# Two tiles at a time to VectorE: handing out the exponentials of an attention kernel in pairs behind group 560

## The chip, the cores and the metric

The kernel runs on one core of one Trainium2 chip. The metric is the device time of one execution in microseconds (us); of several executions the median is given. The core's engines are TensorE (PE in the profile; PEld is its weight load), ScalarE (ACT), VectorE (DVE), GpSimd (POOL) and SyncE (SP, which here issues most DMAs). They run side by side and wait for one another on semaphores only.

## The reference

The input `x` (2048 rows of 512) goes through two branches, and a gate mixes them:

```python
x = A_x
g = _sigmoid((x * gate_w).sum(-1, keepdims=True))
a = _A_ref(x, A_wqkv, A_wo)          # softmax attention, 32 heads of 16
b = _B_ref(x, B_A_re, ..., B_Dskip)  # long convolution with a kernel K(d, l) of 512 x 2048
return g * a + (1 - g) * b
```

The attention is the part that matters here:

```python
scores = jnp.einsum("bhqd,bhkd->bhqk", q, k) * scale
p = _softmax(scores, axis=-1)
o = jnp.einsum("bhqk,bhkd->bhqd", p, v)
```

It has 32 x 2048 x 2048 scores, each of which needs an exponential. The convolution branch builds its kernel K from powers of complex numbers, in 16 blocks of 32 channels, and applies it with matmuls.

## The kernel before, in words

**Tiles, quads, groups.** The scores are cut into 2048 tiles of 128 keys by 512 queries. Four tiles that share the keys and queries and differ in the head make a *quad* (512 quads; 16 quads make a block, 32 blocks). A list `tiles` gives the order in which tiles are worked on, and three consecutive entries are a *group*: 683 groups, the unit of the main loop at the end of `record`. A group's three tiles lie in the three banks of one of two PSUM buffers, `SC0` and `SC1`, which take turns: group g uses `SC[g % 2]`.

**One group's way.** `qk(g)` has TensorE write the three tiles of scores into `SC[g % 2]` (line 701, shown as `SC<-Qm,KT`). `ex(g)` has ScalarE take the exponential of the group, in one ACTIVATE over three tiles (1536 columns) or two (1024), into the ring `ET` or `EX` in SBUF (line 961). `pv(q)` then multiplies a finished quad with the values into the bank `OA`. As there are two buffers, `qk(g + 1)` can start only when group g - 1 has been read out of its buffer, and ScalarE can start group g + 1 only when `qk(g + 1)` is done.

**VectorE's share.** Some groups give their third tile to VectorE. Such a tile is turned into a 16-bit pattern that, read as bfloat16, approximates the exponential (`bits`, line 982, shown as `DZ<-SC`). Three shifted copies of that pattern (`batch`, line 996, shown as `DU<-DZ`, the shifts are in `CUTS`) are summed with it by matmuls (`sums`), which evens the error out. Four tiles of one quad are a *set*: a set covers three quads, of which one (c in the code) goes to VectorE and two (a and b) to ScalarE. Its four VectorE tiles lie in four consecutive groups, one in each, so that ScalarE has four groups of two tiles. The dictionary `vec` holds, for each such group, the number of its set and which of the set's four tiles it has.

**What sets the order.** All of this is planned in Python while the program is built. `Prog` keeps a clock for each engine from a cost given with each instruction; `Sched` holds threads of work (projections, tables of the convolution kernel, its application, outputs) and puts pieces of them between the groups where the clocks leave room. The order on each engine's queue is fixed by this plan. `decide` chooses where a set starts: at a group x, and, behind the last set's start, at a distance of at least 5 groups (the `gap` in `WIN`), or at least 9 (`SL`) where the plan counts as *slow*. It is slow when fewer blocks of the convolution kernel are finished than a line in x asks for:

```python
def win(x):
    slow = done() < KA + (x - KX) / KB
    return next((w for w, (lo, hi, _, gap, *_) in enumerate(WIN) if lo <= x < hi and x >= plan["x"] + (SL if slow else gap)
                 and len(sets) <= (min(x, XR) - RX) / RATE + max(x - XR, 0) / RATE2), None)
```

`done()` is the number of finished blocks (99 once all 16 are finished), `KA` is -2, `KX` is 100 and `KB` is 26. With k blocks finished the plan is slow at groups beyond 100 + (k + 2) x `KB`. A set also starts only in the first 13 quads of a block. `WIN` has two windows: groups 110 to 559 (window 0) and 560 to 677 (window 1); they differ in the number of buffers for VectorE's results.

The finished blocks are seen in the profile by the transposition `Kt<-MB` (line 1402), one for each block. The outputs of rows 0 to 1535 (`MB<-Wo,OnR`, and line 1618) come after the last block has been applied. What follows the last group is a fixed chain: the last quad, normalisation, the last output rows, their DMA.

Of the kernel before, what the change touches and what calls it, by code (L numbers as in the profile page):

```python
# [11 lines left out]
ALU = mybir.AluOpType  # L12
# [37 lines left out]
XS = 128 * DH ** -.5 / math.log(2)  # L50
CUTS = (26, 56, 94)
XB = 128 * (127 - math.log2(5.3794))
# [5 lines left out]
KX = 100  # L58
SL = 9
YQ = 0  # L60
KB = 26
RX = 100
RATE2 = 5.3
XR = 560
# [30 lines left out]
SPILL = 3  # L95
DVCAP = 6
DVK = 14
JS = ((2, 0, 3, 1), (1, 0, 2, 3), (0, 2, 1, 3))
DVL = 14
VW = 136  # L100
VG = 4 * VW + 16
# [2 lines left out]
class Buf:  # L104
# [18 lines left out]
    def int(self, off, dims):  # L123
        return self(off, dims).bitcast(INT32)
# [12 lines left out]
class Prog:  # L137
# [113 lines left out]
    def op(self, eng, fn, R=(), W=(), c=.1, lat=.085, a=0, cfg=None):  # L251
        if self.cap is not None:
            self.cap.append((self.op, (eng, fn, R, W), dict(c=c, lat=lat, a=a, cfg=cfg)))
            return
        if cfg is not None:
            if cfg != self.cfg:
                c += TURN[cfg]
            self.cfg = cfg
        self.act += a
        self.log.append((self.op, self.q, (eng, fn, R, W)))  # L260
        deps = self._deps(eng, R, W)
        i = self.cnt[eng]
        at = self.tm[eng]
        for s, k in deps.items():
            at = max(at, self.fin[(s, k)] + (.03 if s == eng else .05))
        if eng == "PE" and len(self.pt) + 1 >= self.edge():
            at = max(at, self.land())
        self.tm[eng] = at + c
        if eng == "DVE":
            self.busy += c  # L270
        self.fin[(eng, i)] = at + c + lat
        self.cnt[eng] += 1
        w = self._record(eng, fn, deps, eng, i, R, W)
        if eng == "PE":
            b = self.edge()
            self.pt += [at] * (2 + max(w - 1, 0))
            if len(self.pt) > b:
                self.av.append(max(self.pt[b - LEAD] + F1, self.av[-1] + F2))
        return at + c + lat
# [406 lines left out]
def record(nc, p, B, ins):  # L686
# [5 lines left out]
    op, dma = p.op, p.dma  # L692
# [128 lines left out]
    tiles, sets, vec, home, held = [], [], {}, {}, {}  # L821
# [3 lines left out]
    def idle():  # L825
        return max(p.tm["ACT"], p.tm["DVE"]) - p.busy
# [9 lines left out]
    def decide(g):  # L836
        while len(tiles) < min(3 * g + 3, NSL):
            q, x = plan["q"], len(tiles) // 3
            kt = q % 16
            if kt == 0:  # L840
                plan["wait"] = None
            plan["used"] = max(plan["used"], idle() - DVCAP)
            if kt < DVK - 1 and win(x) is not None and idle() - plan["used"] >= WIN[win(x)][4] \
                    and (kt < DVL or not sets or f"dvp{len(sets) - 1}" in sch.flag):
                w = win(x)
                plan["used"] += WIN[w][4]
                plan["x"] = x
                c = q if kt else q + 1
                a, b = [y for y in range(q, q + 3) if y != c]
                own, late = [4 * a + k for k in range(4)] + [4 * b + k for k in range(4)], [4 * c + k for k in JS[len(tiles) % 3]]  # L850
                js = JS[len(tiles) % 3]
                k = 0
                for _ in range(12):
                    if len(tiles) % 3 == 2:
                        vec[len(tiles) // 3] = (len(sets), k)
                        k += 1
                        tiles.append(late.pop(0))
                    else:
                        tiles.append(own.pop(0))
                plan["wait"] = f"dvp{len(sets)}"  # L860
                n = sum(st["w"] == w for st in sets)
                r, ru = f"{w}{n % WIN[w][2]}", f"{w}{n % WIN[w][5]}"
                old = [i for i, st in enumerate(sets) if st["r"] == r]
                olu = [i for i, st in enumerate(sets) if st["ru"] == ru]
                sets.append(dict(js=js, q=c, b=c // 16, w=w, r=r, ru=ru, z=B["DZ" + r], u=[B[f"DU{ru}{k}"] for k in range(len(CUTS))],
                                 old=old[-1] if old else None, olu=olu[-1] if olu else None))
                qs, plan["q"] = [a, b], q + 3
            else:
                tiles.extend(range(4 * q, 4 * q + 4))
                qs, plan["q"] = [q], q + 1  # L870
            for y in qs:
                if y < NQ - 1:
                    todo.append((y, plan["prev"], plan["wait"]))
                plan["prev"] = y
            seat()
            while todo and 4 * todo[0][0] + 3 in home:
                sch.add(pvq(*todo.pop(0)), 0)

    def seat():
        while 3 * len(held) + 3 <= len(tiles) or len(tiles) == NSL and len(held) < NG:  # L880
            g = len(held)
            n = 2 if g in vec else len(slots(g))
            m = NS2 if g >= NSG else NS
            if plan["at"] < NS < plan["at"] + n:
                plan["at"] = NS
            if plan["at"] + n > m:
                plan["at"] = 0
            held[g] = plan["at"]
            for i in range(n):
                home[tiles[3 * g + i]] = held[g] + i  # L890
            plan["at"] = (held[g] + n) % m
# [23 lines left out]
    def at_slot(s):  # L915
        q, j = divmod(tiles[s], 4)
        b, kt = divmod(q, 16)
        return q, j, b, kt, (b % 8) // 2

    def slots(g):  # L920
        return range(3 * g, min(3 * g + 3, NSL))
# [33 lines left out]

    def ex(g):
        sc, e = SC[g % 2], held[g]
        ts = tiles[3 * g:3 * g + (2 if g in vec else 3)]
        n = len(ts)
        E, at = et(e)  # L960
        op("ACT", lambda a: a.activation(E(at, [[1, 512 * n]]), sc(0, [[1, 512 * n]]), AF.Exp, scale=DH ** -0.5),  # L961
           [(sc, i, g) for i in range(n)], [(E, e + i, ts[i]) for i in range(n)] + [(B["tk"], g)], c=.055 + .4267 * n, lat=.105)
        p.tick = max(g - 1, 0)
# [12 lines left out]
            pv_mm(s, *et(home[s]), [(et(home[x])[0], home[x], x) for x in (own if k == 0 else [s])], QUAD if k == 0 else 0)  # L976

    def bits(g):
        i, k = vec[g]
        sc, z = SC[g % 2], sets[i]["z"]  # L980
        yield ("DVE", .6, -1)
        op("DVE", lambda v: v.tensor_scalar(z.u16(512 * k, [[1, 512]]), sc(1024, [[1, 512]]), XS, XB, ALU.mult, ALU.add),  # L982
           [(sc, 2, g)], [(z, k, (i, k))], c=.605)
        sch.mark(f"bits{g}")
        if k == 3:
            sch.add(batch(i), 0)

    def batch(i):
# [705 lines left out]
    for q4 in range(4):  # L1694
        sc = SC[1] if q4 < 3 else MB
# [44 lines left out]
    lack = t0 = bare = 0  # L1740
    for g in range(NG):
        p.q = g
        for i in range(2 if g in vec else len(slots(g))):
            if held[g] + i in ring:
                sch.force(f"pv{ring[held[g] + i] // 4}")
            ring[held[g] + i] = tiles[3 * g + i]
        ex(g)
        sch.mark(f"g{g}")
        sch.mark(f"blk{at_slot(3 * g)[2]}")
        if g + 1 < NG:  # L1750
            decide(g + 1)
            need(g + 1)
            if g - 1 in vec:
                sch.force(f"bits{g - 1}")
            sc = SC[(g + 1) % 2]
            while lack >= 256 and bare:
                n = 512 if lack >= 512 else 256
                for j in range(4):
                    zero((sc, [(sc, 0, ("z", g + 1))]), n, (0, 32 * j), 128, 32, n * ZCOL if j == 0 else 0, n // 4, "C", True)
                lack -= n  # L1760
                bare -= 1
            lack += p.act
            qk(g + 1)
            if g + 1 in vec:
                i = sets[vec[g + 1][0]]["old"]
                if i is not None:
                    sch.force(f"dvp{i}")
                sch.add(bits(g + 1), 0)
        t = p.tm["ACT"]
        want = (FILL if g < REST[3] else FILL2) * (t - t0) / 1.335 + min(max(lack, -256), 768)  # L1770
        t0 = t
        sch.rest = g < REST[3] and g % REST[0] < REST[1]
        if sch.rest:
            want = max(want, REST[2])
        sch.fill(t, t + OVER, want)
        lack = want - p.act
        p.act = bare = 0
        while lack >= 256 and p.tm["PE"] < t + OVER and g < NG - 1:
            z = zbank()
            if z is None:  # L1780
                bare = BARE
                break
            n = 512 if lack >= 512 else 256
            for j in range(4):
                zero(z, n, (0, 32 * j), 128, 32, n * ZCOL if j == 0 else 0, n // 4, "C")
            lack -= n
        p.act = 0
# [27 lines left out]
    for i in range(4):  # L1815
        b, off, sl = banks[i]
# [42 lines left out]
```

## Time and profile before

| | |
|---|---|
| median of 3 runs | 786.94 us (786.87 to 787.43) |
| profiled execution, its own time | 787.2 us |
| its span in the profile | 785.4 us |
| mean granted TensorE clock | 0.997 |
| ScalarE busy | 768.4 us, 98% of the span |
| VectorE busy | 748.7 us, 95% |
| TensorE busy | 689.5 us, 88% |
| VectorE's conversions of score tiles | 372 (93 sets of four) |

The profile is of one execution. A row of the grouped views gives a line, an engine, an operation, what it writes and reads, and the number of instructions, then busy time and the mean duration of one. Where consecutive instructions of ScalarE or VectorE run without a pause, the record of one begins before that of the one before it has ended, so that durations add up to more than the time that passed; the time that one costs is then the distance between two ends.

### The profile page before, as it was taken

The numbers are of one execution on the slowest core, as the hardware profiler recorded it, in microseconds if no ns is written. First come the engines' busy times: TensorE is split into PE (matmuls) and PEld (weight loads), VectorE is DVE, ScalarE is ACT, GpSimd is POOL, SyncE is SP. The second block draws the span as 40 slices with busy tenths as digits, with TensorE's granted clock in tenths as the row PEclk, the third lists the DMA queues.
The fourth block names the chain that finished last, engine by engine and source line by source line (L and its number), as shares of the span: only waits on it lengthen the run. The fifth ranks groups of instructions, "written<-read, shape, count | busy, mean of one in ns | idle before, by whom it ended". The sixth has DMA issues, their size and how long they took to land.

```text
span 785.4 us, 31633 instructions
## 1 busy us (share of the span) xinstructions
PE 689.5 (88%) x14177; PEld 295.3 (38%) x14177; DVE 748.7 (95%) x1307; ACT 768.4 (98%) x694; POOL 11.5 (1%) x21
## 2 busy tenths in 40 slices
PE   7787778788778999989999899989999999889997
PEld 3233332222224544445444455443444444322222
DVE  7999998999999999999999999999999999899996
ACT  7999999999999999999999999999999999999996
POOL 5000000000000000000000000000000000000000
PEclk9999999999999999999999999999999999999999
DMA  9544212302002677674776664775665588721101
GB/s 201 90 108 89 62 40 92 116 31 59 5 8 53 158 178 189 162 205 105 195 177 178 194 158 111 206 193 165 178 143 140 136 194 210 174 48 32 32 15 35
DMA packets 168425, 95.52 MB, mean 122 GB/s; under 512 B 117729, under 2 KB 148834, under 8 KB 167906
## 3 DMA queue, kind: packets, MB, share of 16 engines
q1 hardware_dynamic: 166274, 92.33, 46.1%
q8 instruction: 111, 1.82, 1.0%
q10 hardware_dynamic: 2016, 1.18, 0.7%
q14 instruction: 24, 0.20, 0.1%
HBM read 63.81 MB, written 19.42 MB: 106 GB/s over the span
## 4 chain that ended last, share of the span: by engine, by line
ACT 91%; PE 4%; DVE 3%; DMA 1%; issue 0%; ACTq 0%; DVEq 0%
ACT ET L961 83%; ACT EX L961 8%; PE SC L701 2%; PE OA L701 1%; PE MB L701 1%; DVE DZ L982 1%; DMA Wk<-in_A_wqkv_dram 1%; DVE DU L996 1%; DVE T L1040 0%; DVE Yst L1497 0%; DVE OT L1016 0%; ACTq L705 0%; DVEq L663 0%; DVE KT L798 0%; DVE Kt L1402 0%
## 5 line engine op out<-in xcount | busy, mean ns | idle before, releaser
L961 ACT ACTIVATE ET<-SC 128x1024 bf16<-128x1024 f32 (+1 forms) x614 | 695.7, 1463 | 4.5 <-PE SC L701 3.3
L701 PE MATMUL SC<-Qm,KT 32*128 32x512 bf16 x2048 | 273.4, 385 | 81.2 <-ACT ET L961 70.6
L982 DVE TENSOR_SCALAR DZ<-SC 128x512 uint16<-128x512 f32 x372 | 248.5, 683 | 13.3 <-PE SC L701 11.3
L996 DVE TENSOR_SCALAR DU<-DZ 128x2048 uint16<-128x2048 uint16 x279 | 183.0, 686 | 0.5
L701 PEld LDWEIGHTS SC<-Qm,KT 32*128 32x128 bf16 x2048 | 70.4, 91 | 275.5 <-ACT ET L961 219.0
L701 PE MATMUL OA<-wm 128*32 128x256 bf16 (+3 forms) x862 | 157.3, 340 | 1.2 <-DVE wm L754 1.2
L701 PE MATMUL OA<-ET,VE 128*32 128x512 bf16 x1516 | 158.1, 390 | 0.2
L701 PE MATMUL OA<-DU,VE 128*32 128x512 bf16 x1116 | 105.0, 385 | 0.0
L701 PEld LDWEIGHTS MB<-U,H 128*32 128x32 bf16 x4096 | 83.0, 144 | 22.6 <-issue 11.8
L701 PE MATMUL MB<-U,H 128*32 128x128 bf16 (+7 forms) x4096 | 87.5, 224 | 0.0
L961 ACT ACTIVATE EX<-SC 128x1024 bf16<-128x1024 f32 (+1 forms) x69 | 81.6, 1406 | 0.0
L701 PEld LDWEIGHTS OA<-ET,VE 128*32 128x32 bf16 x1516 | 40.8, 94 | 75.5 <-issue 72.0
L1040 DVE TENSOR_TENSOR T<-B,DT 128x1536 bf16<-128x1536 bf16 x64 | 59.3, 947 | 0.0
L701 PEld LDWEIGHTS MB<-T,Z 128*32 128x32 bf16 x2048 | 46.1, 153 | 12.3 <-issue 7.0
L701 PE MATMUL MB<-T,Z 128*32 128x64 bf16 (+1 forms) x2048 | 48.6, 235 | 0.1
L701 PEld LDWEIGHTS OA<-wm 128*32 128x32 bf16 (+2 forms) x862 | 41.8, 95 | 14.5 <-issue 11.4
L701 PEld LDWEIGHTS OA<-DU,VE 128*32 128x32 bf16 x1116 | 28.8, 96 | 33.9 <-issue 24.2
L701 PE MATMUL OA<-DZ,VE 128*32 128x512 bf16 x372 | 37.2, 384 | 1.0 <-issue 1.0
L1016 DVE STREAM_TRANSPOSE OT<-OA 128x512 f32<-128x512 f32 x32 | 22.7, 709 | 2.8 <-PE OA L701 2.8
L1497 DVE TENSOR_TENSOR Yst<-MB,gt 128x512 bf16<-128x512 f32 x32 | 21.8, 682 | 2.2 <-PE MB L701 1.9
L701 PE MATMUL OA<-EX,VE 128*32 128x512 bf16 x160 | 21.9, 387 | 0.0
L1040 DVE TENSOR_TENSOR ft<-Z,DM 128x1024 bf16<-128x1024 bf16 x32 | 21.3, 676 | 0.0
(145 smaller groups left out, 439.6 us busy)
## 6 DMA issues: line engine op xcount, KB each, us to landing
H<-gm_kd SPq DMA_DIRECT2D x128, 256.0 KB, 3.8
U<-gm_xs SPq DMA_DIRECT2D x128, 134.2 KB, 3.5
T<-B SPq DMA_DIRECT2D x16, 256.0 KB, 3.1
gm_yd<-Yst SPq DMA_DIRECT2D x64, 64.0 KB, 2.9
gm_bd<-B16s SPq DMA_DIRECT2D x3, 1024.0 KB, 4.5
B<-gm_bd SPq DMA_DIRECT2D x12, 256.0 KB, 4.0
gm_kd<-Ks SPq DMA_DIRECT2D x64, 40.0 KB, 3.2
gm_xs<-xP SPq DMA_DIRECT2D x16, 136.0 KB, 3.4
```

Of the source, the lines that this page charges most:

```text
L701: op("PE", lambda t: t.matmul(out(), lhsT(), rhs(), start=start, stop=stop, skip_group_check=True, **kw), R, W, c=c, lat=.15, a=a, cfg=cfg)
L961: op("ACT", lambda a: a.activation(E(at, [[1, 512 * n]]), sc(0, [[1, 512 * n]]), AF.Exp, scale=DH ** -0.5), [(sc, i, g) for i in range(n)] ...
L982: op("DVE", lambda v: v.tensor_scalar(z.u16(512 * k, [[1, 512]]), sc(1024, [[1, 512]]), XS, XB, ALU.mult, ALU.add), [(sc, 2, g)], [(z, k, ...
L996: op("DVE", lambda v, u=u, cut=cut: v.tensor_scalar(u.u16(0, [[1, 2048]]), z.u16(0, [[1, 2048]]), float(cut), None, ALU.add), R, [(u, 0, i ...
L1016: op("DVE", lambda v: v.transpose(OT(512 * w, [[1, 512]]), OA(0, [[1, 512]])), [(OA, 0, b)], [(OT, w, b)], c=.64)
L1040: op(eng, lambda v: v.tensor_tensor(o(), a(), b_(), f), R, W, c=c)
L1497: op("DVE", lambda v, w=w, h=h: v.tensor_tensor(Yst(1024 * w + 4 * h, [[128, R8], [8, 16], [1, 4]]), MB(0, [[1, R8], [R8, 16], [NC, 4]]), ...
```

## The change

Sets in window 1, which starts at group 560, use new patterns of tiles (`PAIRED`). A pattern lists the set's twelve tiles in their order; there are three, for a set that starts at the first, second or third place of a group. In each of them VectorE's four tiles lie in two groups, two in each, in the second and third bank, and one ACTIVATE of one tile (512 columns) is left to ScalarE there. The set's other groups have three tiles for ScalarE. `bits` converts the two tiles in one instruction over 1024 columns, and its planned cost is a formula in the number of tiles (0.604 us for one in place of 0.605). In window 0 the patterns (`SINGLE`) spell out the order that was there before. Apart from that `KB` goes from 26 to 26.6, which moves the line against which the finished blocks are counted, in both windows.

```diff
-KB = 26
+KB = 26.6
...
-JS = ((2, 0, 3, 1), (1, 0, 2, 3), (0, 2, 1, 3))
+SINGLE = ("a0 a1 c2 a2 a3 c0 b0 b1 c3 b2 b3 c1", "a0 c1 a1 a2 c0 a3 b0 c2 b1 b2 c3 b3", "c0 a0 a1 c2 a2 a3 c1 b0 b1 c3 b2 b3")
+PAIRED = ("a0 c1 c2 a1 a2 a3 b1 c0 c3 b0 b2 b3", "c0 c1 a1 a2 a3 a0 c2 c3 b0 b1 b2 b3", "a0 a1 c0 c2 a2 a3 b1 b0 c1 c3 b2 b3")
+RUN = (SINGLE, PAIRED)
...
-                own, late = [4 * a + k for k in range(4)] + [4 * b + k for k in range(4)], [4 * c + k for k in JS[len(tiles) % 3]]
-                js = JS[len(tiles) % 3]
-                k = 0
-                for _ in range(12):
-                    if len(tiles) % 3 == 2:
-                        vec[len(tiles) // 3] = (len(sets), k)
-                        k += 1
-                        tiles.append(late.pop(0))
-                    else:
-                        tiles.append(own.pop(0))
+                js, at = [], {}
+                for t in RUN[w][len(tiles) % 3].split():
+                    if t[0] == "c":
+                        at.setdefault(len(tiles) // 3, []).append(len(js))
+                        js.append(int(t[1]))
+                    tiles.append(4 * dict(a=a, b=b, c=c)[t[0]] + int(t[1]))
+                for y, ks in at.items():
+                    vec[y] = (len(sets), ks[0], len(ks))
...
-            n = 2 if g in vec else len(slots(g))
+            n = act(g)
...
+    def act(g):
+        return 3 - vec[g][2] if g in vec else len(slots(g))
+
...
-        ts = tiles[3 * g:3 * g + (2 if g in vec else 3)]
+        ts = tiles[3 * g:3 * g + act(g)]
...
     def bits(g):
-        i, k = vec[g]
+        i, k, n = vec[g]
         sc, z = SC[g % 2], sets[i]["z"]
-        yield ("DVE", .6, -1)
-        op("DVE", lambda v: v.tensor_scalar(z.u16(512 * k, [[1, 512]]), sc(1024, [[1, 512]]), XS, XB, ALU.mult, ALU.add),
-           [(sc, 2, g)], [(z, k, (i, k))], c=.605)
+        yield ("DVE", .07 + .534 * n, -1)
+        op("DVE", lambda v: v.tensor_scalar(z.u16(512 * k, [[1, 512 * n]]), sc(512 * (3 - n), [[1, 512 * n]]), XS, XB, ALU.mult, ALU.add),
+           [(sc, 3 - n + x, g) for x in range(n)], [(z, k + x, (i, k + x)) for x in range(n)], c=.07 + .534 * n)
         sch.mark(f"bits{g}")
-        if k == 3:
+        if k + n == 4:
             sch.add(batch(i), 0)
```

More of the change, by code (lines that the diff above doesn't have):

```diff
@@ L1742, in record @@
         p.q = g
-        for i in range(2 if g in vec else len(slots(g))):
+        for i in range(act(g)):
             if held[g] + i in ring:
```

## The prediction

> **What bounds the kernel now.** I read the page first: its head, the busy times, the chain that ended last.
>
> ```profile
> span 785.4 us, 31633 instructions
> PE 689.5 (88%) x14177; PEld 295.3 (38%) x14177; DVE 748.7 (95%) x1307; ACT 768.4 (98%) x694; POOL 11.5 (1%) x21
> ACT 91%; PE 4%; DVE 3%; DMA 1%; issue 0%; ACTq 0%; DVEq 0%
> ```
>
> ScalarE is busy 98% and has 91% of the chain; VectorE is close behind at 95%. The chain in order of time (start, length, what) gives the price of one ACTIVATE, as pieces in which ScalarE never waits:
>
> ```profile
> 11.92 1.45 ACT ET L961
> ...
> 13.89 69.84 ACT ET L961 x52
> ...
> 603.15 0.59 DVE DZ L982
> 603.79 0.40 PE SC L701
> 604.21 4.20 ACT ET L961 x4
> ...
> 624.05 1.20 DVE DZ L982 x2
> ...
> 700.37 2.75 ACT EX L961 x3
> ```
>
> The piece of 52 lies before group 110, where all groups have three tiles: 69.84 / 52 = 1.343 us each. The piece at 700.37 is three groups of two tiles: 2.75 / 3 = 0.917. A tile more costs 0.426, so one tile alone should cost 0.917 - 0.426 = 0.491. The first ACTIVATE, with none before it, took 1.45: running on, each saves some 0.10. The grouped rows give the number of each form:
>
> ```profile
> L961 ACT ACTIVATE ET<-SC 128x1536 bf16<-128x1536 f32 x288 | 414.8, 1720 | 2.4 <-PE SC L701 2.2 <-PE OA L701 0.2
> L961 ACT ACTIVATE ET<-SC 128x1024 bf16<-128x1024 f32 x326 | 330.0, 1236 | 2.1 <-PE SC L701 1.1 <-PE OA L701 0.9
> L982 DVE TENSOR_SCALAR DZ<-SC 128x512 uint16<-128x512 f32 x372 | 248.5, 683 | 13.3 <-PE SC L701 11.3
> L961 ACT ACTIVATE EX<-SC 128x1024 bf16<-128x1024 f32 x47 | 51.4, 1270 | 0.0
> L961 ACT ACTIVATE EX<-SC 128x1536 bf16<-128x1536 f32 x22 | 35.1, 1697 | 0.0
> ```
>
> 310 groups of three and 373 of two. The first ends at 11.92 + 1.45 = 13.37; the others cost 309 x 1.343 + 373 x 0.917 = 757.0. Now by stages: from 13.37 to group 110, window 0, window 1, and what follows the last ACTIVATE (us, then busy us of each engine):
>
> ```profile
> 13.37:161.00 147.63, 115.93 (x2286) 43.22 (x2290) 141.68 (x265) 146.87 (x111) 0.32 (x1) 0.99 0.38 90
> 161.00:650.00 489.00, 442.36 (x10001) 207.81 (x9993) 475.87 (x815) 486.14 (x451) 0.00 (x0) 1.00 0.54 141
> 650.00:776.56 126.56, 116.70 (x1772) 38.18 (x1765) 118.87 (x195) 126.56 (x124) 0.00 (x0) 1.00 0.32 79
> 776.56:785.38 8.82, 4.42 (x23) 1.51 (x21) 3.58 (x7) 1.07 (x2) 0.00 (x0) 0.91 0.18 60
> ```
>
> So the span is 13.37 + 757.0 + 8.82 and 6.2 us in which ScalarE starved. The third row matters most: where the new patterns go, ScalarE is busy for all of 126.56 us, and VectorE (the third busy figure, 118.87) has 7.7 us to spare. There time can be won only by giving ScalarE fewer columns, and is lost by any wait of ScalarE.
>
> **The change part by part.** *ScalarE's own work in window 1.* Four of the 372 conversions make a set, 93 sets in all. Of the stretch from 650.00 to 776.56 alone:
>
> ```profile
> L961 ACT ACTIVATE ET<-SC 128x1024 bf16<-128x1024 f32 x63 | 67.4, 1321 | 0.0
> L982 DVE TENSOR_SCALAR DZ<-SC 128x512 uint16<-128x512 f32 x92 | 61.9, 685 | 5.7 <-PE SC L701 4.8
> ```
>
> That is 23 sets (one starts every 5.33 groups in 118, as close as the gap allows, so no further set fits in). A set cost 4 x 0.917 = 3.67 us and will cost 2 x 0.491 + 2 x 1.343 = 3.67: nothing won, nothing lost.
>
> *A wait it adds.* With two buffers, the scores of group g + 1 are written between the end of group g - 1 and the start of g + 1, that is, while ScalarE works on g. From the timeline, at 699 to 701 us:
>
> ```profile
> 699.03 1.34 ACT L961 ACTIVATE ET<-SC 128x1024 bf16<-128x1024 f32 x1
> ...
> 700.42 0.09 PEld L701 LDWEIGHTS SC<-Qm,KT 32*128 32x128 bf16 x1 [0.47 <-ACT ET L961]
> 700.43 0.39 PE L701 MATMUL SC<-Qm,KT 32*128 32x512 bf16 x1
> ```
>
> The ACTIVATE ends at 700.37; the matmuls start 0.06 later and take 0.39; TensorE had stood idle for 0.47, waiting for just this end. In the chain above, matmuls that end at 604.19 release ScalarE at 604.21, 0.02 later (0.04 with the rounding of the rows). So group g + 1 starts 0.47 to 0.49 after the end of g - 1. Over a group of two tiles (0.917) that leaves 0.4 us. Behind the change each group of one tile is followed by one of three (in all three patterns), and one tile lasts 0.491: the next ACTIVATE starts just as that one ends, takes the 1.45 of one that runs alone instead of 1.343, and ScalarE loses (0.47 to 0.49) + 1.45 - 0.491 - 1.343 = 0.09 to 0.11 us. Two such places in each of 23 sets: 46 x 0.10 = 4.6 us, all on the path that ends last. The bounds: nothing, if ScalarE takes a late start without loss; and 0.3 a place (13.8) if TensorE is also busy with one more batch (0.39 long, issued in about 0.2) when the buffer comes free. I take 0.10, as TensorE's idle 0.47 says that it is there in time.
>
> The Trainium skill ("ScalarE: Activation LUTs", section "What ACT_TABLE_LOAD costs") states 186 ns + 0.833 ns per column for an ACTIVATE, and that back-to-back ones overlap by about 93 ns. By that, one tile costs 0.520 in a row instead of my 0.491, the loss is 0.49 + 0.093 - 0.520 = 0.06 a place, an estimate of 2.8 us for the 46. Its two figures fit three tiles alone (1.466 for a measured 1.45) but miss the distance in a row (1.373 for 1.343), so I stay with the rows; the direction is the same.
>
> *VectorE's work.* Two conversions in a row take 1.20 (the row at 624.05). For 1024 columns the nearest rows are float products of 1024 and 512 columns:
>
> ```profile
> L1040 DVE TENSOR_TENSOR ft<-FP,L 128x1024 f32<-128x1024 f32 x8 | 9.6, 1219 | 0.0
> L1040 DVE TENSOR_TENSOR ft<-FP,L 128x512 f32<-128x512 f32 x8 | 5.2, 677 | 0.0
> ```
>
> 512 columns more cost 0.54, so a pair in a row costs 0.60 + 0.54 = 1.14 and saves 0.06, 46 x 0.06 = 2.8 us of VectorE; the bounds are 0 and, were the second half as cheap as the copies over 2048 16-bit columns (0.60), 0.6 a pair. It lies in the stretch where VectorE has 7.7 us to spare and ScalarE none: worth nothing to the time. The other side: a buffer now comes free only when VectorE has read its two tiles. Its instruction can start with the scores, some 0.5 after the end of g - 2, and ends 1.2 later, at 1.7; ScalarE's next need of this buffer (0.49 before the end of g + 1, less the 0.10) is at 1.343 + 0.491 + 1.343 - 0.59 = 2.6. A wait behind one other instruction (0.6 to 0.75) is covered; a wait behind two (1.2) costs some 0.3. I take none.
>
> *KB.* With k blocks of the convolution kernel done, the plan turns slow 0.6 x (k + 2) groups later: 1 to 10 groups. Each set that this brings turns four groups of three into four of two: 4 x 0.426 = 1.70 us less for ScalarE, against 4 x 0.60 conversions and 3 x 0.60 shifted copies, 4.2 us, more for VectorE. That work delays the blocks that the rule counts, and so calls the slow plan back. The last block shows how tight the rule is:
>
> ```profile
> L1402 DVE STREAM_TRANSPOSE Kt<-MB x16: 694/706/718, 248.8 to 628.2; 128x512 f32<-128x512 f32 x16
> ```
>
> Its sixteenth and last record is the last block's. The stretch up to it, for line 961 alone (busy us of ScalarE and the number of its ACTIVATEs):
>
> ```profile
> 0.00:628.20 628.20, 613.88 (x541) 1.00 0.51 129
> ```
>
> So 541 ACTIVATEs have begun by then; the bound for it is 100 + 17 x 26 = 542 and becomes 552.2. The blocks may thus run up to ten groups late. At full density (a set in 5.33 groups, 4 x 0.917 + 1.33 x 1.343 = 5.5 us, 4.2 of them for the set) ten groups leave VectorE 10 x 1.3 / 5.33 = 2.4 us; in a slow stretch (a set in 9, 10.4 us, 6.2 left) 6.9 us. The work put off is 2.4 to 6.9 us, room for 0.6 to 1.6 sets. I take one, 1.7 us; the ends are none and two, and three if VectorE's 13 us of idle time in window 0 can be used. The tables put off by ten groups move their stores, loads and the output matmuls with them; these outputs are through early:
>
> ```profile
> L701 PE MATMUL MB<-Wo,OnR x192: 378/379/391, 697.4 to 763.5; 128*32 128x512 bf16 x192
> ```
>
> 13 us before the last ACTIVATE ends: covered, and beyond that each us late would be a us lost. Nothing else moves: SP, POOL and DMA issues keep their order, and one-tile sets of window 0 keep their instructions.
>
> *The sum.* 787.2 of the profiled execution + 4.6 - 1.7 = 790.1. The median, 786.94, lies 0.26 below that execution: 789.8.
>
> **The rivals.** *The added sets come back to none* (the delayed blocks bring one slow gap more): + 4.6, 791.5. For it: 541 against 542, the rule is a loop. Against it: ten groups of leeway.
>
> *Two sets*, 788.1; *three or more*, 786.4. For it: VectorE's idle 13 us; against it: it is idle in scraps.
>
> *The wait does not form*, the one on the other side: ScalarE takes up group g + 1 while g still runs, and a start 0.1 too late costs nothing, so that the sets alone count: one gives 786.94 - 1.7 = 785.2, faster. It decides where a place costs under (1.70 - 1.57) / 46, practically nothing. For it: ACTIVATEs overlap in the records (the first at 699.03 lasts 1.34 for a cost of 0.917). Against it: the 1.45 of one that starts behind an empty engine.
>
> *VectorE frees the buffer late* in a third of the pairs, 15 x 0.35 = 5 us more: 795. For it: it is busy 94% in window 1. Against it: the 0.9 us of slack, of which one instruction ahead takes 0.75 at most.
>
> The Trainium skill ("VectorE: DVE Perf Modes", section "The TRN2 errata — SBUF-src ops pay a fixed extra latency per instruction") has 120 + columns cycles at 0.96 GHz for a read from PSUM, and advises large tiles, as each pays the fixed part once: 1.19 for a pair instead of 2 x 0.66, an estimate of 5.8 us of VectorE for the 46. It speaks for the change where VectorE sets the end; by the third stage row it does not.
>
> **How the numbers follow.** Chances: the forecast 0.35 (its own range 788.7 to 791); no added set 0.19; two 0.16; three or more 0.07; no wait 0.15; VectorE late 0.08. A change under 0.2% (1.6 us) can hardly be told from none. Faster: 0.15. Within: 0.16 + 0.07 = 0.23. Slower: 0.35 + 0.19 + 0.08 = 0.62. Leaving out the last case and the upper edge of the second, the range is 785.0 to 792.3.
>
> **What would show it.** 46 ACTIVATEs of 128x512, each followed by one of 1536 that lasts about 1.45 where it lasted 1.7, and with its end 1.44 behind the one before; ScalarE's idle or lost time behind group 560 up from under 1 to about 5 us; VectorE's conversions of 1024 columns at 1.2 alone; 376 tiles converted in all (94 sets). It is wrong if those ACTIVATEs end 1.343 apart, if the number of sets differs from 94 by two or more, or if the time before group 560 grows because blocks of the convolution kernel come late.

## The result, and the profile after

The changed kernel takes 796.06 us (794.46 to 800.11, four runs) against 786.9 us: 1.26% slower, ratio 1.0126 with an interval of 1.0103 to 1.0149. A second set of four runs, on another occasion, gave 797.51 us and 1.0144 (1.0128 to 1.0161). The forecast was slower, 789.8 us, with a range up to 792.3; the direction was right, and the step that it forecast is a third of the one that came.

The profiled execution is the slowest of the first four, 800.11 us, with a span of 798.3. Its page, in the lines that answer to those shown of before:

```profile
span 798.3 us, 31726 instructions
PE 695.7 (87%) x14199; PEld 296.4 (37%) x14199; DVE 746.3 (93%) x1261; ACT 774.3 (97%) x694; POOL 11.4 (1%) x21
ACT 77%; PE 10%; DVE 8%; DMA 3%; issue 2%; ACTq 0%; SPq 0%; DVEq 0%
```

ScalarE has as many instructions as before (694), and its share of the chain that ended last falls from 91% to 77%, while TensorE's rises from 4% to 10% and VectorE's from 3% to 8%: ScalarE now waits for others. The grouped rows by form:

```profile
L964 ACT ACTIVATE ET<-SC 128x1536 bf16<-128x1536 f32 x321 | 454.0, 1654 | 7.1 <-PE SC L703 6.1
L964 ACT ACTIVATE ET<-SC 128x1024 bf16<-128x1024 f32 x260 | 257.2, 1182 | 2.0 <-PE SC L703 1.6 <-PE OA L703 0.3
L985 DVE TENSOR_SCALAR DZ<-SC 128x512 uint16<-128x512 f32 x280 | 186.5, 683 | 12.6 <-PE SC L703 10.9
L985 DVE TENSOR_SCALAR DZ<-SC 128x1024 uint16<-128x1024 f32 x46 | 56.5, 1228 | 11.2 <-PE SC L703 10.8
...
L964 ACT ACTIVATE ET<-SC 128x512 bf16<-128x512 f32 x29 | 17.6, 607 | 0.0
L964 ACT ACTIVATE EX<-SC 128x512 bf16<-128x512 f32 x17 | 10.2, 601 | 0.0
```

29 + 17 = 46 ACTIVATEs of one tile, 46 conversions of two. VectorE converted 280 + 2 x 46 = 372 tiles: 93 sets, as before, not 94. So ScalarE's work by the prediction's prices is the same sum in both kernels, 757.0 us, and nearly the whole difference is waiting. To see where, the span is cut at the end of group 559. A row is a stretch of the trace: its start, end and length in us, the busy time of PE, PEld, DVE, ACT and POOL (with the number of instructions), the granted clock, the busy share of the DMA engines and their GB/s. Before:

```profile
13.37:650.33 636.96, 558.62 (x12283) 251.03 (x12283) 617.89 (x1079) 633.34 (x562) 0.32 (x1) 1.00 0.51 130
650.33:776.56 126.23, 116.37 (x1768) 38.18 (x1765) 118.54 (x195) 126.23 (x124) 0.00 (x0) 1.00 0.32 79
```

After:

```profile
13.10:654.19 641.09, 561.31 (x12072) 246.64 (x12072) 616.28 (x1076) 634.32 (x562) 1.22 (x5) 0.99 0.50 124
654.19:790.11 135.92, 120.50 (x2006) 44.08 (x1998) 117.70 (x152) 131.16 (x124) 0.00 (x0) 1.00 0.38 97
790.11:798.31 8.20, 4.20 (x22) 1.50 (x20) 3.58 (x7) 1.07 (x2) 0.00 (x0) 1.00 0.20 65
```

From group 560 on, ScalarE has 30 x 1.343 + 93 x 0.917 = 125.6 us of work before, and 46 x 0.491 + 76 x 1.343 + 0.917 = 125.6 after. It took 126.2 before and 135.9 after: 0.7 us of waits have become 10.3. Ahead of group 560 the work is 757.0 - 125.6, or 631.5 with one decimal more; waits of 5.5 us have become 9.6. The tail (what follows the last ACTIVATE) is 0.6 shorter, the start 0.3. That is 9.7 + 4.1 - 0.9 = 12.9, the distance of the two spans.

A *place* from here on is a group of one tile and the group of three behind it. Two places in a row, from the timeline of the kernel after:

```profile
696.96 2.55 ACT L964 ACTIVATE EX<-SC 128x512 bf16<-128x512 f32 x3
697.12 0.09 PEld L703 LDWEIGHTS SC<-Qm,KT 32*128 32x128 bf16 x1 [0.68 <-ACT ET L964]
...
699.08 0.10 PEld L703 LDWEIGHTS SC<-Qm,KT 32*128 32x128 bf16 x3 [0.20 <-ACT EX L964]
699.08 0.39 PE L703 MATMUL SC<-Qm,KT 32*128 32x512 bf16 x3
699.52 4.13 ACT L964 ACTIVATE ET<-SC 128x1536 bf16<-128x1536 f32 x3
```

The row at 696.96 holds three ACTIVATEs, of one tile, three tiles and one tile, and ends at 699.51. The ACTIVATE of three in its middle releases the matmuls of 699.08; they end at 699.47, and the next ACTIVATE of three starts at 699.52, 0.01 behind the end of the tile that was to hide them. The chain in order of time shows the same as lengths:

```profile
697.07 0.49 ACT EX L964
697.57 1.94 ACT EX L964 x2
...
711.33 3.28 ACT ET L964 x3
...
723.00 1.14 DVE DZ L985
```

One tile costs 0.49; a start behind an idle engine and one tile 1.94 = 1.45 + 0.49; a start, one of three in a row and one tile 3.28 = 1.45 + 1.34 + 0.49. These prices of the prediction stand, and so does VectorE's 1.14 for a pair (the row at 723.00).

Of 45 such places (all but the window's first), 31 find TensorE ready (scores start 0.054 to 0.069 us behind the end that releases them). There the usual loss is 0.11 to 0.125 us; three have 0.2 more because the ACTIVATE itself took 1.65 to 1.67, for which no cause was found. In the other 14 TensorE comes late, 4.3 us in all. So the 10.3 us are 46 x 0.12 = 5.5 at every place, 4.3 of a late TensorE and 0.6 of long ACTIVATEs. One place has half of the lateness:

```profile
690.86 1.16 PEld L703 LDWEIGHTS MB<-U,H 128*32 128x32 bf16 x59 [0.23 <-issue]
...
693.36 0.43 PEld L703 LDWEIGHTS MB<-U,H 128*32 128x32 bf16 x21 [1.34 <-issue]
...
693.84 0.10 PEld L703 LDWEIGHTS SC<-Qm,KT 32*128 32x128 bf16 x3
...
694.28 1.45 ACT L964 ACTIVATE ET<-SC 128x1536 bf16<-128x1536 f32 x1 [2.02 <-PE SC L703]
```

A long run of the convolution's small matmuls (`MB<-U,H`) stood ahead of the scores on TensorE's queue, and within it TensorE paused for 1.34 us without any wait that the profile shows ("issue"). The six late places up to 692 us all have such `MB<-U,H` matmuls ahead of the scores and make up 3.5 of the 4.3 us.

### The profile page after: what moved, and what is told of

It reads as the page before. It is cut to its first block, busy times and chain, and to the rows that moved or that the text cites. A ratio compares the mean times of both kernels' runs of the same rounds, so it can differ in the third digit from the quotient of the medians.

```text
span 798.3 us, 31726 instructions
## 1 busy us (share of the span) xinstructions
PE 695.7 (87%) x14199; PEld 296.4 (37%) x14199; DVE 746.3 (93%) x1261; ACT 774.3 (97%) x694; POOL 11.4 (1%) x21
## 4 chain that ended last, share of the span: by engine, by line
ACT 77%; PE 10%; DVE 8%; DMA 3%; issue 2%; ACTq 0%; SPq 0%; DVEq 0%
ACT ET L964 71%; ACT EX L964 6%; PE SC L703 4%; PE OA L703 3%; DVE DZ L985 3%; PE MB L703 3%; DMA H<-gm_kd 2%; DVE DU L999 1%; DVE T L1043 1%; DMA Wk<-in_A_wqkv_dram 1%; DVE Yst L1500 1%; DVE ft L1043 0%; DVE OT L1019 0%; DVE fo L1621 0%; DVE Z L1043 0%
## 5 line engine op out<-in xcount | busy, mean ns | idle before, releaser
L964 ACT ACTIVATE ET<-SC 128x1536 bf16<-128x1536 f32 (+2 forms) x610 | 692.8, 1403 | 9.1 <-PE SC L703 7.7
L985 DVE TENSOR_SCALAR DZ<-SC 128x512 uint16<-128x512 f32 (+1 forms) x326 | 242.9, 760 | 23.8 <-PE SC L703 21.7
L703 PE MATMUL OA<-wm 128*32 128x256 bf16 (+3 forms) x884 | 160.3, 349 | 1.2 <-DVE wm L756 1.2
L703 PE MATMUL MB<-U,H 128*32 128x128 bf16 (+7 forms) x4096 | 89.3, 224 | 2.0 <-issue 1.2
L964 ACT ACTIVATE EX<-SC 128x1536 bf16<-128x1536 f32 (+2 forms) x73 | 79.4, 1161 | 2.5 <-PE SC L703 2.4
L703 PEld LDWEIGHTS MB<-T,Z 128*32 128x32 bf16 x2048 | 45.5, 154 | 11.8 <-issue 7.5
L703 PE MATMUL MB<-T,Z 128*32 128x48 bf16 (+1 forms) x2048 | 48.0, 235 | 0.4 <-issue 0.4
L703 PE MATMUL OA<-EX,VE 128*32 128x512 bf16 x164 | 24.0, 389 | 0.3 <-ACT ET L964 0.3
```

The source lines that it names most:

```text
L703: op("PE", lambda t: t.matmul(out(), lhsT(), rhs(), start=start, stop=stop, skip_group_check=True, **kw), R, W, c=c, lat=.15, a=a, cfg=cfg)
L985: op("DVE", lambda v: v.tensor_scalar(z.u16(512 * k, [[1, 512 * n]]), sc(512 * (3 - n), [[1, 512 * n]]), XS, XB, ALU.mult, ALU.add), [(sc, ...
```

## The experiments

The theory at this point (waiting theory) is that the one-tile groups cost what the timeline shows; the rival is that the shifted `KB` has spoilt the plan before group 560 and the pairs cost only the fixed part.

**The pairs alone.**

```diff
-KB = 26.6
+KB = 26
...
-        yield ("DVE", .07 + .534 * n, -1)
+        yield ("DVE", .6 if n == 1 else 1.138, -1)
...
-           ... c=.07 + .534 * n)
+           ... c=.605 if n == 1 else 1.138)
```

> The pairs alone: KB back at 26 and the planned cost of a conversion of one tile back at 0.605, so that the plan up to group 560 is that of the kernel before. Waiting theory (each of the 46 groups of one tile makes ScalarE wait 0.12 us for the next scores, and more where TensorE comes late): 5.4 us fixed and 2 to 3 us for a late TensorE, so 7 to 9 us over the kernel before, nearly all of the change's 9. Rival (the new KB has spoilt the plan of window 0, and the pairs cost only the fixed part): 4.5 to 5.5 us.

Measured: 793.67 us against 786.31, ratio 1.0089 (1.0067 to 1.0112), 7.4 us by the medians. From its trace:

```profile
12.69:649.01 636.32, 558.61 (x12283) 250.40 (x12283) 618.10 (x1079) 633.41 (x562) 0.20 (x1) 1.00 0.52 130
649.01:782.18 133.17, 117.13 (x1806) 40.58 (x1803) 116.56 (x149) 131.06 (x123) 0.00 (x0) 1.00 0.29 76
```

Behind group 560, 133.2 for 125.6 us of work: 7.6 us of waits, of which 46 x 0.12 = 5.5 are fixed and 1.7 come from a late TensorE (10 places). Ahead of it the order is that of before, and so, within 0.7 us, is the time. This is the waiting theory's number; it is not quite the whole loss of the change, though.

**KB alone**, the patterns of before in both windows. The planned cost of a conversion stays that of the change (0.604), too:

```diff
-RUN = (SINGLE, PAIRED)
+RUN = (SINGLE, SINGLE)
```

> The changed kernel with the single patterns in both windows, so that only KB = 26.6 and the 1 ns of planned cost are left; 93 sets. Waiting theory: within 1.5 us of the kernel before, as the number of sets is the same and ScalarE's work with it. Rival (KB has spoilt window 0): 3 to 4.5 us slower.

Measured: 790.85 us, 1.0054 (1.0034 to 1.0075), 4.5 us slower, with 93 sets. Here the rival is right. The stages:

```profile
13.16:652.13 638.97, 558.51 (x12072) 245.90 (x12072) 616.38 (x1076) 633.68 (x563) 1.22 (x5) 0.99 0.50 124
652.13:778.51 126.38, 117.89 (x1941) 41.30 (x1937) 119.96 (x198) 126.26 (x123) 0.00 (x0) 1.00 0.40 102
778.51:788.81 10.30, 5.75 (x42) 2.12 (x43) 3.58 (x7) 1.07 (x2) 0.00 (x0) 1.00 0.19 64
```

2.0 us more of waits ahead of group 560 than in the profile of before, and a tail that is 1.5 us longer. The largest piece of the waits lies at groups 534 to 542: 3.7 us, where the kernel before waited 0.6.

```profile
628.02 0.55 PEld L703 LDWEIGHTS MB<-U,H 128*32 128x32 bf16 x32 [1.22 <-DMA H<-gm_kd]
...
629.05 1.02 ACT L964 ACTIVATE ET<-SC 128x1024 bf16<-128x1024 f32 x1 [1.75 <-PE SC L703]
```

TensorE waited 1.22 us for a transfer of the convolution kernel (`H<-gm_kd`), with the matmuls that need it ahead of the next scores on its queue, and ScalarE then waited 1.75 for these scores. Table work stood on TensorE's queue before its data had come. The run with fewer outputs, which has the same order there, lost 3.5 us at the same groups.

Now the tail. The last block's table comes at 640.0 in place of 628.2 and the output matmuls run to 775.8 in place of 763.5:

```profile
L1405 DVE STREAM_TRANSPOSE Kt<-MB x16: 673/708/717, 248.5 to 640.0; 128x512 f32<-128x512 f32 x16
```

```profile
L703 PE MATMUL MB<-Wo,OnR x192: 379/379/390, 713.8 to 775.8; 128*32 128x512 bf16 x192
```

What they hold up is seen at the end, where the last copy of a late output (`fo<-MB`, on VectorE behind the last set's shifted copies) keeps the bank `MB` from the final output rows:

```profile
777.72 0.69 DVE L1625 CAST fo<-MB 128x512 bf16<-128x512 f32 x1
...
778.46 0.34 PEld L703 LDWEIGHTS MB<-Wo,OnT 128*32 128x32 bf16 x12 [0.57 <-DVE fo L1625]
```

**One pair in a set** instead of two, in the pairs alone (half the places, same columns, same number of ACTIVATEs):

```diff
-PAIRED = ("a0 c1 c2 a1 a2 a3 b1 c0 c3 b0 b2 b3", "c0 c1 a1 a2 a3 a0 c2 c3 b0 b1 b2 b3", "a0 a1 c0 c2 a2 a3 b1 b0 c1 c3 b2 b3")
+PAIRED = ("a0 c1 c2 a1 a2 a3 b0 b1 c3 b2 b3 c0", "c0 c1 a1 a2 a3 a0 b1 c2 b0 b2 c3 b3", "c1 a1 c0 c2 a2 a3 a0 b0 b1 c3 b2 b3")
```

> As the pairs alone, but each set of window 1 has one pair and two single tiles: 23 groups of one tile in place of 46, with ScalarE's columns and the number of its instructions unchanged (0.49 + 1.34 + 2 x 0.92 a set). Waiting theory: half of the loss of the pairs alone, 2.7 us fixed and 1 to 1.5 for a late TensorE, so 3.5 to 4.5 us over the kernel before. Rival (the loss comes from VectorE's long instruction holding the buffer now and then, or from the new order as a whole): no proportion to the number of places, near 0 or near the full 7 to 9.

Measured: 788.74 us, 1.0027 (1.0014 to 1.004), 2.4 us.

```profile
649.53:778.69 129.16, 116.68 (x1776) 38.76 (x1774) 117.23 (x172) 128.88 (x123) 0.00 (x0) 1.00 0.32 79
```

129.2 for 125.6: 3.6 us of waits, of which the 22 places between two groups of the window have 3.25 us, 0.15 each. The loss goes with the number of places. The time lies under the 3.5 us expected, as TensorE was late at one place only, by 0.05.

**TensorE earlier.** In the pairs alone, the other work of TensorE ahead of the scores behind a one-tile group is planned to end earlier:

```diff
-        sch.fill(t, t + OVER, want)
+        over = -.2 if g + 1 in vec and act(g + 1) == 1 else OVER
+        sch.fill(t, t + over, want)
...
-        while lack >= 256 and p.tm["PE"] < t + OVER and g < NG - 1:
+        while lack >= 256 and p.tm["PE"] < t + over and g < NG - 1:
```

> As the pairs alone, but TensorE's other work ahead of the scores that follow a group of one tile is planned to end 0.2 us before ScalarE's planned end in place of 0.3 behind it. Waiting theory: the part that comes from a late TensorE (2 to 3 us) goes or shrinks to under 1, the fixed part stays: 5.5 to 6.5 us over the kernel before, and places where the scores start more than 0.1 us behind the end of ScalarE's instruction go from some 15 to under 5. Rival (TensorE's lateness is of no weight): the same time as the pairs alone.

Measured: 795.07 us, 1.0106 (1.0091 to 1.0121), 8.8 us over the kernel before. The expectation fell. The waits behind group 560 are 8.1 us, not 6. TensorE is late at 6 places instead of 10, but by 1.5 us in all instead of 1.7, and 0.9 us are lost elsewhere. So the margin of the plan decides where TensorE is late and hardly how much. And the tail grew to 10.5 us, as the output matmuls, pushed back, ran to 779.9.

**The hole, and its control.** If ScalarE really has nothing to do for 0.12 us at each place, it must be able to do something there for nothing. A small ACTIVATE was put behind each one-tile ACTIVATE of the pairs alone, planned at no cost; the control has it in the kernel before, behind 46 ACTIVATEs of two tiles.

```diff
+    sb("dm", 16)
...
         ex(g)
+        if g >= 560 and g in vec and act(g) == 1:
+            op("ACT", lambda a: a.activation(B["dm"](0, [[1, 16]]), wm(0, [[1, 16]]), AF.Exp, scale=DH ** -0.5), [(wm, 0)], [(B["dm"], 0)], c=0, lat=.1)
```

In the control the condition is `g >= 560 and g in vec and vec[g][1] % 2 == 0`.

> As the pairs alone, with a small instruction of no use to the result (an exponential of 16 columns of zeros, planned at no cost, so that the plan is the same) put on ScalarE right behind each of the 46 ACTIVATEs of one tile. Waiting theory: ScalarE has 0.12 us of nothing to do there, so the instruction falls into the hole: at most 1.5 us over the pairs alone, whatever it costs elsewhere up to some 0.12 each. Rival (the place costs 0.12 because an ACTIVATE of one tile has a higher fixed cost, with ScalarE at work all the time): the full price of 46 such instructions on top, 2 us at 0.05 each, 5.5 at 0.12.

> The kernel before with the same small instruction behind 46 of its ACTIVATEs of two tiles in window 1 (behind the first and third group of each set). It gives the price of the instruction where ScalarE has no hole: by both theories 46 times 0.05 to 0.15, 2 to 7 us over the kernel before.

Measured: with the pairs 793.33 us, 1.0097 (1.0063 to 1.0132), where the pairs alone had 793.67 (the kernel before beside them 786.33 and 786.31); the control 790.67 us, 1.0056 (1.0033 to 1.0079), 4.3 us over the kernel before. The stage behind group 560, with the pairs, and then of the control:

```profile
648.52:781.97 133.45, 117.13 (x1806) 40.82 (x1803) 116.53 (x149) 132.34 (x169) 0.00 (x0) 1.00 0.30 75
```

```profile
648.30:779.07 130.77, 116.89 (x1767) 38.05 (x1765) 119.60 (x195) 130.77 (x170) 0.00 (x0) 1.00 0.31 77
```

133.45 instead of 133.17 with the pairs, 130.77 instead of 126.23 in the control: the same 46 instructions cost 0.3 us in one and 4.5 (0.10 each) in the other. The order of all other work on ScalarE and VectorE is unchanged in both. So the 0.12 us of a place is an empty engine and not a price of short ACTIVATEs.

**What KB does.** `KB` alone on the kernel before, and then the planned cost alone, which the change also moves by a thousandth of a microsecond (and by four where a thread announces it):

```diff
-KB = 26
+KB = 26.6
```

> The kernel before with KB = 26.6 and nothing else: its plan has 92 sets, one fewer than before. Plan theory (KB moves the order of work before group 560, and ScalarE's columns by the number of sets): 1.7 us from the set, and waits of ScalarE for TensorE or VectorE in window 0 of some 2 us more than before, 2 to 5 us slower. Rival (the step to the KB-alone run came from the 1 ns of planned cost): under 2 us slower.

```diff
-        yield ("DVE", .6, -1)
+        yield ("DVE", .604, -1)
...
-           [(sc, 2, g)], [(z, k, (i, k))], c=.605)
+           [(sc, 2, g)], [(z, k, (i, k))], c=.604)
```

> The kernel before with only the planned cost of a conversion changed, 0.605 to 0.604 us (0.600 to 0.604 where the thread announces it). Nothing that runs on the chip has another form, but the plan comes out with 91 sets in place of 93. Plan theory: two sets fewer are 2 x 1.70 us for ScalarE, so 3.4 us slower, 2.5 to 5 with other waits. Rival (the plan's clock does not matter that far): within 1 us of the kernel before.

Measured: 792.88 us, 1.0085 (1.0053 to 1.0117), and 792.37 us, 1.0081 (1.0055 to 1.0107). The grouped row of conversions, of the one and of the other:

```profile
L982 DVE TENSOR_SCALAR DZ<-SC 128x512 uint16<-128x512 f32 x368 | 245.8, 683 | 19.2 <-PE SC L701 17.1
```

```profile
L982 DVE TENSOR_SCALAR DZ<-SC 128x512 uint16<-128x512 f32 x364 | 244.0, 684 | 21.3 <-PE SC L701 19.4
```

They are 6.6 and 6.0 us over the kernel before, both above the 5 us at which the expectations end. The sets are 92 and 91: 1.7 and 3.4 us by ScalarE's columns, the rest are waits. A planned cost that is a few nanoseconds off, with not one instruction of another form, makes this kernel 0.8% slower. Each of the changes tried that moves the plan before group 560 ends worse than the plan of before; none of the four plans (the change, KB with the cost, KB, the cost) had more than 93 sets.

**Fewer late outputs.** To see what lengthened the tail in the run with KB alone, a part of the late outputs was left out there.

```diff
-        for lt in range(13):
+        for lt in range(4, 13):
```

> The run with KB alone (single patterns, 93 sets), but without the last matmuls, the copy and the store of output rows 0 to 511, which are left out: a third of the outputs that come late there. In that run 10.3 us lay between the end of the last ACTIVATE and the end of the span, against 8.8 before. Late-outputs theory: the tail goes back to 8.8 us or less, and the time falls by 1.5 us, to some 3 us over the kernel before; the waits of ScalarE in window 0 stay. Rival (the tail has another cause, such as the last set or the order of the last groups): the tail stays at 10.3 us.

Measured: 789.43 us, 1.0048 (1.0029 to 1.0067), and the tail:

```profile
779.29:787.82 8.53, 4.41 (x22) 1.51 (x21) 3.58 (x7) 1.07 (x2) 0.00 (x0) 1.00 0.19 63
```

The kernel leaves out the last step of output rows 0 to 511. The tail is 8.5 in place of 10.3, as the late-outputs theory has it. By the times the two runs can't be told apart (1.0048 and 1.0054); the profile carries this verdict. In the changed kernel itself the tail is short (8.2): there the outputs' matmuls end at 778.1, 12 us before the last ACTIVATE, which the pairs have delayed. Alone, the two parts of the change cost 7.4 + 4.5 = 11.9 us by the medians; together they cost 9.2 us in the first set of runs and 11.6 in the second, so whether they add up in full stays open.

**The changed kernel again.**

> The changed kernel itself once more, for a second profile and for a comparison on the chip beside the others. Waiting theory: 46 places at 0.12 us and 2 us of late TensorE again behind group 560; the waits before group 560 (8.9 us in the first profile, where TensorE's granted clock was at half for some 10 us) come out lower where the clock stays up: 8 to 10 us over the kernel before. Rival (the waits before group 560 are fixed by the plan): 8.9 us of them again.

Measured: 797.51 us against 785.96, 1.0144; the profiled execution took 800.08. Its stages:

```profile
13.92:653.35 639.43, 559.64 (x12072) 246.72 (x12072) 615.92 (x1076) 633.61 (x562) 1.22 (x5) 0.99 0.51 124
653.35:790.07 136.72, 121.09 (x2005) 44.19 (x1998) 117.64 (x152) 131.19 (x124) 0.00 (x0) 0.99 0.38 95
```

11.1 us of waits behind group 560 and 8.0 ahead, where the first profile had 9.6 by the sum above (the expectation's 8.9 was too low). The time is 11.6 us over the kernel before, more than the 8 to 10 expected, as TensorE was late by 4.9 us and not by 2. The waits ahead go with the plan's order. From the end of the first ACTIVATE to the end of group 559 the four executions with the new order (changed kernel twice, KB alone, fewer outputs) took 639.0 to 641.1 us, the six with the old order (before, the pairs alone and what is built on it, the control) 635.3 to 637.0. Each of the four also has a stretch of half clock between 300 us and the end of group 559 (the last section shows some), and none of the six. The pause at the same run of small matmuls is there again (1.46 us), and the pairs alone had 1.7 us of a late TensorE. The difference lies in the table work: with the later blocks the `MB<-U,H` matmuls reach to 703.5 us in the changed kernel and end at 675.8 in the pairs alone, so more of them meet one-tile groups, which have no slack for them:

```profile
L703 PE MATMUL MB<-U,H x4096: 197/220/273, 265.2 to 703.5; 128*32 128x128 bf16 x25, 128*32 128x88 bf16 x25, 128*32 128x112 bf16 x25, 128*32 128x72 bf16 x25
```

```profile
L703 PE MATMUL MB<-U,H x4096: 206/220/272, 265.5 to 675.8; 128*32 128x128 bf16 x25, 128*32 128x88 bf16 x25, 128*32 128x112 bf16 x25, 128*32 128x72 bf16 x25
```

Why TensorE pauses in these runs for over a microsecond was not tried; the profile names no releaser. One lead from the traces: a packet of 16 KB on the queue `instruction` ended at 692.03 us, as the pause began, and at 690.87 in the second execution; TensorE went on 1.33 and 1.38 us later. But most such packets behind group 560 are followed by no pause, so this is not shown to be the cause. No version faster than the kernel before came out of this: pairs cost ScalarE waits and win time only on VectorE, which does not set the end behind group 560.

## Why the prediction was wrong, by its steps

Two steps failed: the term for KB, by its sign, and the term for the wait, by its size. The forecast has - 1.7 and + 4.6; the profile has + 4.1 ahead of group 560 and + 9.7 behind it, of which some 2.6 come with the new order, too, as the lateness of TensorE goes from 1.7 to 4.3.

- *What bounds the kernel.* Right: in the kernel before, ScalarE has 0.7 us of idle time behind group 560, and what VectorE saves there brought nothing.
- *ScalarE's own work in window 1, unchanged.* Right: 0.49 and 1.34 in the chain, 125.6 us in both.
- *A wait it adds, 46 x 0.10 = 4.6 us.* The mechanism was right in each link, and the hole experiment shows it. The size was low twice. A place costs 0.12, not 0.10, since the scores take 0.395 and ScalarE starts 0.05 behind them (I had 0.39 and 0.02 to 0.04): 5.5 us. And "TensorE's idle 0.47 says that it is there in time" was wrong: it was read off from one typical place. TensorE is late at 10 places with the pairs alone, by 1.7 us in all, and at 14 in the changed kernel, by 4.3 (4.9 in the second execution). By the prices, a group of two tiles has some 0.3 us of slack for such delays (0.917 less the 0.5 from one buffer's release to the start on it and the 0.1 of the start-up); one-tile groups have none. The upper bound of 13.8 us for this term had it inside, the range of the forecast did not.
- The Trainium skill's figures for ACTIVATE ("ScalarE: Activation LUTs", section "What ACT_TABLE_LOAD costs"), by which the place would have cost 0.06, are further off than the rows: 0.12 was measured.
- *VectorE's work.* Right: 1.14 for a pair, and it never held a buffer: in the first profile of the changed kernel all of window 1's waits of ScalarE but 0.1 us lie at the places behind one-tile groups. The rival of a late VectorE is out.
- *KB, one set more, - 1.7 us.* This step failed, and by its sign. The sets came to 93 (92 with KB and nothing else), and the new plan costs 4.5 us where it stands alone: waits of ScalarE ahead of group 560 and, without the pairs, a longer tail. I had priced the sets that a rule allows and taken the order of the work between them for given. But the change of KB and of the planned cost gave another order from about group 205 on, and the old one had fewer waits. Why the plan found no further set was not traced. The prediction's own sign of being wrong came: the changed kernel reaches the end of group 559 at 654.2 us instead of 650.3, with the last block's table at 642.1 instead of 628.2. "Covered" for late outputs was wrong too: with KB alone the tables came 11.8 us later, the outputs 12.3 us, against a cover of 13, and the tail grew by 1.5, since the copies behind the outputs wait for VectorE, which the cover had left out.
- Of the rivals, *no added set* (791.5) was nearest in its mechanism, and short by the late TensorE and by the waits ahead of group 560. *VectorE late* (795) was nearest in its number, by luck, as what it describes did not happen. That ScalarE takes a late start without loss is refuted. The direction came right although one of the two terms had the wrong sign.

## What to carry to other kernels

With two buffers that take turns, the shortest instruction of the bounding engine must be longer than the refill (release, matmuls, release back: 0.055 + 0.395 + 0.05 us here) and the start-up that it otherwise overlaps (0.10) together; equal sums of work are not equal time if one piece falls below that. Slack that the profile shows as idle time of another engine (0.3 us at each two-tile group) may be what swallows that engine's occasional delays; look at its late places, not at its typical one. And where a planner sets the order, a change of its constants is a change of the whole order: cost the plan it makes, or keep its clock as it was.

## What the runs showed of the hardware

TensorE's granted clock falls to half for stretches of 3.41 or 6.83 us. Two from the changed kernel, each below the row of the 3.4 us ahead of it (columns as above: busy times of PE, PEld, DVE, ACT and POOL, then the clock and DMA):

```profile
321.69:325.10 3.41, 2.89 (x36) 1.00 (x33) 3.41 (x7) 3.07 (x4) 0.00 (x0) 1.00 0.49 143
325.10:331.93 6.83, 6.67 (x54) 1.47 (x52) 6.04 (x9) 5.22 (x4) 0.00 (x0) 0.50 0.85 176
...
604.99:608.41 3.42, 1.57 (x50) 0.91 (x47) 2.53 (x6) 2.29 (x3) 0.00 (x0) 1.00 0.66 178
608.41:611.82 3.41, 3.41 (x27) 0.50 (x23) 2.27 (x4) 2.52 (x3) 0.00 (x0) 0.50 0.50 131
```

The run with KB alone has one behind the wait for `H<-gm_kd`:

```profile
625.90:629.31 3.41, 1.95 (x75) 1.32 (x75) 1.75 (x3) 1.66 (x3) 0.00 (x0) 1.00 0.73 201
629.31:632.73 3.42, 3.42 (x63) 1.08 (x55) 2.92 (x6) 2.74 (x3) 0.00 (x0) 0.50 0.56 151
```

In the last two TensorE was busy for about half of the time ahead (1.57 and 1.95 us), with pauses of 1.85 and 1.10 us. In the first it was busy for 2.89 of 3.41 us, so a long pause is not needed, and why the clock fell there stays open. Nor does the clock fall each time: from 130 to 132 us TensorE is busy for 1.11 us in the kernel before and for 1.07 in the run with one pair; in the first the clock is at 0.50 in the next 2 us, in the second at 1.00.

The Trainium skill ("TensorE: Matmul & The Clock Gate", section "Part 1: The HAM clock gate (the "warmup" mystery)") states that the clock is either full or half and falls after an idle window of about 3.4 us. The two levels agree (0.50 and 1.00), and the stretches are 3.41 us long or twice that; but the pauses ahead of them are shorter here, 1.85 us at most in the three shown.

In such a stretch the scores take 0.61 us in place of 0.39, and ScalarE waits for them:

```profile
609.76 0.61 PE L703 MATMUL SC<-Qm,KT 32*128 32x512 bf16 x3
...
610.41 1.02 ACT L964 ACTIVATE EX<-SC 128x1024 bf16<-128x1024 f32 x1 [0.51 <-PE SC L703]
```

Around the two stretches of the changed kernel's first profile ScalarE lost some 5 of the 9.6 us that it waited ahead of group 560 (groups 262 to 266 and 517 to 520); 1.2 of them, at group 517, are from the pause itself, before the clock fell. The second profile has its stretches elsewhere, at 353.5 to 356.9 and at 694.8 to 698.2 us. So a part of the loss differs from one execution to the next; the first four runs of the changed kernel lie 5.7 us apart.
